# Sparse attention and an ELU layer on one core: scores without padded k, two tiles for q^T and k^T, fillers in batch 0, a new order

## The chip, the core and the metric

The kernel runs on one core of a Trainium2 chip. The core has a matrix engine (TensorE, in profiles PE, with its weight loads as PEld), a vector engine (DVE), a scalar engine (ACT), GpSimd (POOL), a queue engine (SP) and 16 DMA engines. The metric is the time of one execution on the device in microseconds (us); lower is better.

## The reference

Attention over 8 batches, 8 heads, 576 tokens of 64 numbers, with two sparse masks, and then a two-layer network with an ELU over all 4,608 tokens:

```python
scores = scale * np.matmul(q, k.transpose(0, 1, 3, 2))
rel = pos[:, None] - pos[None, :]
mask_local = (rel >= 0) & (rel < 32)                       # heads 0 to 3
mask_strided = (rel >= 0) & (pos[None, :] % 32 == pos[:, None] % 32)   # heads 4 to 7
attn = softmax(np.where(mask, scores, -1e9))
x = (attn @ v).transpose(0, 2, 1, 3).reshape(B * S, H * D)   # 4608 x 512
h = x @ w_in                                                 # 512 -> 2048
g = np.where(h > 0, h, np.exp(np.minimum(h, 0)) - 1)
out = g @ w_out                                              # 2048 -> 512
```

q, k, v and both weights come in float32 and are cast to bf16 as they are loaded; the output is float32.

## The kernel before

**Attention.** Each batch has four strided heads (class s) and four local heads (class l). The token axis is cut into 8 residue classes of 72 tokens for s, and into blocks of 96 for l, so that only blocks that the masks leave are computed. A class has two pairs y of two heads, a pair has two halves u. So a batch has 8 score groups: those of s are eight matmuls of 72 columns, those of l six of 96 columns. A group goes through this chain: scores S (TensorE, L438), exp e (ACT, L445), mask m (DVE), product with v O (TensorE), log of the sums n and reciprocal r (ACT), and x, the product written to xT (DVE). The v tile of the later batches holds columns of ones, so O gives the sums as well.

**q^T and k^T.** In batches 0 to 2 TensorE transposes q and k (T), and a copy brings them to SBUF (c on DVE, C on ACT). From batch 3 on (`NPE = 3`) SP's DMA transposes do this (X, L587). The two heads or residues z of a matmul pair lie in partitions 0 to 63 and 64 to 127 of qT and kT. In batches 0 to 2 a score matmul uses only its 64 partitions, so the two z of a pair lie side by side on the array. From batch 3 on there are two copies `kp` of k^T, in each of which the other 64 partitions are zero, and a score matmul uses all 128 partitions. The copies are filled by two DMAs on SP for each class (P, L593); their zeros are written once at the start, by four copies on ACT (L334) and four small memsets. There is one qT and one kT for each class, so the transposes of a batch wait for the scores of the batch before.

**The network.** Tokens are taken in 9 chunks of 512. For each chunk 16 first-layer rows of four 512-column matmuls (L; in chunk 0 two halves a and b) give h in a PSUM bank; h, i or j and g (exp on ACT, clamp on DVE or ACT, ELU on DVE) write g; then 4 second-layer blocks of four parts with four matmuls each (Z), a copy o (ACT) or q (DVE) into one of two output buffers, and the stores t on SP. A chunk needs all x of the batches that it covers: L.1 those of batches 0 and 1, L.2 of 1 and 2, L.5 of 4 and 5, L.6 of 5 and 6.

**The order.** All work is issued in the order of a long string `ORDER`, a token a step; each engine takes its own steps from it in that order. The names are `S.3l0.1.67` (scores of batch 3, class l, pair 0, half 1, in banks 6 and 7), `D.kl.3` (load k of the local heads of batch 3, on POOL's queue), `X.kl.3` (its DMA transpose, on SP's), `L.2.5.0` (chunk 2, row 5, bank 0), `Z.1.3.0.2` (chunk 1, block 3, part 0, bank 2), `W` and `V` (copies of v), `w.7.42` (42 matmuls of zeros of 128 columns into bank 7), `F` (masks) and `K` (casts of the first q and k). The eight PSUM banks are named in the string by hand.

Of the kernel before, what the change touches and what calls it, by code (L numbers as in the profile page):

```python
# [8 lines left out]
F32 = mybir.dt.float32  # L9
BF16 = mybir.dt.bfloat16  # L10
# [5 lines left out]
S = 576  # L16
D = 64
# [30 lines left out]
T.1l1.q.1 g.0.6 h.0.12 T.1l0.q.5 C.1l1.q i.0.1 a.0.9.6 i.0.12 C.1l0.q T.1l1.k.7 g.0.2 T.1l0.k.1
C.1l1.k g.0.12 T.1s1.k.5 b.0.9 C.1l0.k g.0.1 T.1s0.q.7 D.qs.2 h.0.9 V.1 S.1l1.0.12 S.1l0.1.34
e.1l1.0 b.0.13 c.1s0.q c.1s1.k e.1l0.1 S.1s0.0.12 m.1l1.0 a.0.8.7 h.0.13 m.1l0.1 O.1l1.0.34 e.1s0.0  # L50
i.0.9 a.0.11.5 i.0.13 D.ks.2 n.1l1.0 m.1s0.0 S.1s0.1.12 b.0.8 r.1l1.0 g.0.9 e.1s0.1 b.0.11 x.1l1.0
Z.0.0.0.6 h.0.8 m.1s0.1 h.0.11 g.0.13 O.1s0.0.34 i.0.8 O.1s0.1.12 D.ql.2 n.1s0.0 i.0.11 Z.0.0.1.6
g.0.8 r.1s0.0 n.1s0.1 x.1s0.0 a.0.14.0 r.1s0.1 g.0.11 O.1l0.1.34 b.0.14 x.1s0.1 n.1l0.1 Z.0.2.0.5
h.0.14 D.kl.2 r.1l0.1 i.0.14 Z.0.0.2.6 x.1l0.1 g.0.14 S.1s1.1.34 S.1s1.0.12 e.1s1.1 Z.0.2.1.5
e.1s1.0 m.1s1.1 D.vs.2 Z.0.0.3.6 m.1s1.0 D.vl.2 S.1l0.0.34 o.0.0 S.1l1.1.12 Z.0.3.0.0 e.1l1.1 t.0.0
e.1l0.0 O.1s1.0.67 m.1l1.1 O.1s1.1.12 m.1l0.0 n.1s1.0 O.1l1.1.34 r.1s1.0 Z.0.3.1.0 n.1s1.1 x.1s1.0
n.1l1.1 r.1s1.1 T.2s0.q.6 T.2s0.k.7 r.1l1.1 x.1s1.1 Z.0.3.2.0 C.2s0.q x.1l1.1 c.2s0.k T.2l1.q.6
S.2s0.1.34 c.2l1.q T.2l1.k.7 e.2s0.1 S.2s0.0.12 c.2l1.k O.1l0.0.34 e.2s0.0 T.2l0.k.6 m.2s0.1 n.1l0.0
m.2s0.0 S.2l1.1.12 r.1l0.0 T.2l0.q.7 c.2l0.k e.2l1.1 Z.0.3.3.0 x.1l0.0 C.2l0.q m.2l1.1 L.1.0.4 V.2
o.0.3 W.2 t.0.3 S.2l1.0.67 h.1.0 S.2l0.1.01 T.2s1.q.3 e.2l0.1 T.2s1.k.2 i.1.0 Z.0.2.2.5 D.qs.3  # L60
c.2s1.q e.2l1.0 m.2l0.1 D.ks.3 O.2s0.1.01 c.2s1.k Z.0.2.3.5 g.1.0 n.2s0.1 D.vs.3 m.2l1.0 r.2s0.1
S.2s1.0.67 D.ql.3 q.0.2 O.2s0.0.34 e.2s1.0 L.1.3.2 x.2s0.1 t.0.2 n.2s0.0 Z.0.1.0.7 m.2s1.0 h.1.3
r.2s0.0 i.1.3 O.2s1.0.01 Z.0.1.1.7 g.1.3 n.2s1.0 x.2s0.0 Z.0.1.2.7 r.2s1.0 x.2s1.0 L.1.1.6 D.kl.3
O.2l0.1.01 h.1.1 L.1.6.2 n.2l0.1 i.1.1 Z.0.1.3.7 g.1.1 r.2l0.1 h.1.6 L.1.2.3 x.2l0.1 o.0.1 i.1.6
S.2l0.0.01 D.vl.3 h.1.2 L.1.5.7 t.0.1 g.1.6 e.2l0.0 i.1.2 O.2l1.1.56 X.ql.3 h.1.5 g.1.2 S.2s1.1.01
L.1.7.2 n.2l1.1 i.1.5 m.2l0.0 e.2s1.1 L.1.4.3 g.1.5 h.1.7 X.qs.3 m.2s1.1 r.2l1.1 O.2l0.0.01 i.1.7
Z.1.0.0.7 h.1.4 g.1.7 n.2l0.0 L.1.12.4 i.1.4 x.2l1.1 r.2l0.0 X.ks.3 L.1.8.2 g.1.4 h.1.12 O.2s1.1.56
x.2l0.0 h.1.8 Z.1.0.1.7 W.3 n.2s1.1 X.kl.3 O.2l1.0.01 i.1.12 r.2s1.1 Z.1.3.0.3 i.1.8 n.2l1.0 g.1.12
Z.1.3.1.3 x.2s1.1 r.2l1.0 L.1.13.4 g.1.8 D.qs.4 x.2l1.0 L.1.10.5 h.1.13 i.1.13 L.2.4.6 h.1.10 g.1.13
L.2.10.0 i.1.10 h.2.4 g.1.10 j.2.4 L.2.2.4 h.2.10 g.2.4 L.2.0.5 h.2.2 i.2.10 i.2.2 L.1.14.6 h.2.0  # L70
g.2.10 D.ks.4 P.s.3 L.2.8.2 i.2.0 h.1.14 g.2.2 D.vs.4 j.1.14 L.1.9.0 g.2.0 D.ql.4 h.2.8 g.1.14
L.2.3.1 h.1.9 i.2.8 i.1.9 L.2.1.6 h.2.3 g.2.8 j.2.3 L.1.11.5 g.1.9 X.ks.4 h.2.1 g.2.3 L.1.15.4
h.1.11 i.2.1 D.kl.4 i.1.11 S.3s0.0.01 h.1.15 L.2.5.2 g.2.1 e.3s0.0 P.l.3 i.1.15 L.2.6.6 g.1.11 h.2.5
m.3s0.0 S.3s1.1.01 h.2.6 g.1.15 Z.1.0.2.7 e.3s1.1 i.2.6 D.vl.4 O.3s0.0.45 i.2.5 S.3s0.1.01 m.3s1.1
n.3s0.0 Z.1.3.2.3 g.2.5 e.3s0.1 g.2.6 Z.1.0.3.7 r.3s0.0 m.3s0.1 O.3s1.1.01 x.3s0.0 o.1.0 Z.1.3.3.3
X.kl.4 n.3s1.1 O.3s0.1.45 q.1.3 r.3s1.1 S.3s1.0.67 Z.1.1.0.2 n.3s0.1 x.3s1.1 t.1.0 e.3s1.0 Z.1.1.1.2
r.3s0.1 m.3s1.0 P.s.4 S.3l0.1.67 O.3s1.0.01 x.3s0.1 e.3l0.1 Z.1.1.2.2 X.qs.4 n.3s1.0 W.4 Z.1.1.3.2
m.3l0.1 r.3s1.0 O.3l0.1.67 x.3s1.0 o.1.1 S.3l0.0.45 L.2.9.3 t.1.3 n.3l0.1 e.3l0.0 L.2.15.0 t.1.1
r.3l0.1 m.3l0.0 L.2.12.4 h.2.9 x.3l0.1 h.2.15 O.3l0.0.12 i.2.9 h.2.12 L.2.7.7 i.2.15 n.3l0.0 g.2.9
Z.1.2.0.6 h.2.7 i.2.12 D.qs.5 g.2.15 r.3l0.0 L.2.11.3 D.ks.5 i.2.7 x.3l0.0 D.vs.5 Z.2.0.0.5 h.2.11  # L80
g.2.7 L.2.14.2 i.2.11 g.2.12 Z.2.0.1.5 h.2.14 g.2.11 i.2.14 L.2.13.7 g.2.14 S.3l1.0.34 h.2.13
Z.1.2.1.6 X.ks.5 e.3l1.0 i.2.13 S.4s0.1.01 g.2.13 S.4s0.0.34 e.4s0.1 Z.2.0.2.5 m.3l1.0 m.4s0.1
e.4s0.0 O.3l1.0.01 Z.1.2.2.6 n.3l1.0 m.4s0.0 O.4s0.1.34 r.3l1.0 Z.2.0.3.5 n.4s0.1 x.3l1.0 Z.1.2.3.6
r.4s0.1 q.2.0 x.4s0.1 O.4s0.0.01 o.1.2 t.2.0 Z.2.2.0.7 n.4s0.0 Z.2.2.1.7 t.1.2 r.4s0.0 Z.2.2.2.7
x.4s0.0 Z.2.2.3.7 S.3l1.1.01 o.2.2 Z.2.1.0.2 P.l.4 e.3l1.1 Z.2.1.1.2 m.3l1.1 X.ql.4 O.3l1.1.01
S.4s1.1.67 n.3l1.1 Z.2.1.2.2 e.4s1.1 Z.2.1.3.2 r.3l1.1 t.2.2 m.4s1.1 O.4s1.1.67 x.3l1.1 o.2.1
S.4s1.0.45 Z.2.3.0.3 n.4s1.1 X.qs.5 D.ql.5 e.4s1.0 L.3.10.2 r.4s1.1 m.4s1.0 L.3.1.4 h.3.10 x.4s1.1
P.s.5 L.3.0.5 i.3.10 h.3.1 g.3.10 t.2.1 L.3.3.6 h.3.0 i.3.1 D.kl.5 g.3.1 j.3.0 L.3.8.7 h.3.3 g.3.0
L.3.9.4 h.3.8 i.3.3 i.3.8 L.3.4.5 h.3.9 g.3.3 D.vl.5 j.3.9 L.3.13.2 g.3.8 X.kl.5 h.3.4 g.3.9 L.3.7.7
h.3.13 i.3.4 i.3.13 L.3.2.4 D.qs.6 h.3.7 g.3.4 D.ks.6 L.3.11.6 i.3.7 h.3.2 g.3.13 L.3.15.5 i.3.2  # L90
h.3.11 g.3.7 S.5s0.1.12 i.3.11 h.3.15 L.3.14.0 g.3.2 e.5s0.1 L.3.6.7 g.3.11 h.3.14 m.5s0.1 j.3.15
L.3.12.6 i.3.14 h.3.6 g.3.15 L.3.5.1 h.3.12 i.3.6 X.ks.6 g.3.14 S.4l0.0.45 h.3.5 Z.2.3.1.3 g.3.6
e.4l0.0 i.3.5 Z.2.3.2.3 i.3.12 g.3.5 S.5s1.1.45 g.3.12 S.4l0.1.01 e.5s1.1 Z.2.3.3.3 m.4l0.0 m.5s1.1
e.4l0.1 O.4s1.0.45 O.4l0.0.67 o.2.3 W.5 S.4l1.1.01 Z.3.0.0.2 n.4s1.0 m.4l0.1 t.2.3 D.vs.6 e.4l1.1
Z.3.0.1.2 r.4s1.0 m.4l1.1 O.5s0.1.01 n.4l0.0 x.4s1.0 Z.3.2.0.3 n.5s0.1 r.4l0.0 O.4l0.1.45 Z.3.2.1.3
# [615 lines left out]
```

## Time and profile before

| | |
|---|---|
| runs | 325.38, 326.49, 326.8 us; median 326.49 |
| the profiled execution | 326.53 us, its span 324.7 us |
| PE busy | 308.3 us (95% of the span) |
| DVE, ACT, POOL busy | 227.3, 234.3, 72.3 us |
| first and second layer | 576 matmuls of 512 columns each |
| score matmuls of full rows | 160 of 72 columns, 120 of 96 columns |
| score matmuls of half rows | 96 of 72 columns, 72 of 96 columns |
| mean granted clock of TensorE | 0.972 |
| slower clock, by the trace | 0.5 up to 5.9 us, from 9.3 to 23.0 and from 101.5 to 104.9 |

How to read it: times count from the start of the span. The timeline's lines give start and duration in us, engine, line, operation, tiles, partitions, shape and count, and in brackets the idle time before and what ended it. Matmuls are pipelined: the difference of two starts is what one costs, not its duration. The waits' lines give engine, line, what was waited for, the total in us, how often, and the longest. The windows' lines give for each engine the busy time and the count, then the clock granted to TensorE as a share of full speed, the busy share of the DMA engines (above 1 where packets overlap) and GB/s.

### The profile page before, as it was taken

How to read it: one execution, taken by the hardware profiler on the slowest of the kernel's cores; microseconds unless marked ns; L12 is line 12 of the kernel's file. 1: busy time of each engine (PE TensorE's matmuls, PEld its weight loads, DVE VectorE, ACT ScalarE, POOL GpSimd, SP SyncE). 2: the span in 40 equal slices, each digit the busy share in tenths (PEclk: the TensorE clock that was granted, in tenths of full speed). 3: DMA queues.
4: the chain of work that ended last, by engine and by line, in shares of the span. 5: the costliest groups of instructions: out<-in, count | busy, mean ns of one | idle time of the engine just before them, and what ended most of it. 6: DMA issues, size and time to landing. Idle time of an engine off the chain costs nothing.

```text
span 324.7 us, 6422 instructions
## 1 busy us (share of the span) xinstructions
PE 308.3 (95%) x2410; PEld 158.8 (49%) x2410; DVE 227.3 (70%) x449; ACT 234.3 (72%) x407; POOL 72.3 (22%) x99
## 2 busy tenths in 40 slices
PE   6899999999997999999999989999999999999993
PEld 5754546544453455445544544445545444444441
DVE  7759967889994772896679668951699673850900
ACT  6767968897885876878978879944899756742610
POOL 8534200840750200910075027000000000000000
PEclk9559999999997999999999999999999999999999
DMA  8999999799999866997499969742501101112122
GB/s 172 194 206 197 204 206 137 120 184 124 198 165 172 173 116 163 180 150 142 115 189 121 115 168 92 100 115 81 126 2 32 47 19 33 32 29 56 46 67 66
DMA packets 97455, 39.41 MB, mean 121 GB/s; under 512 B 77936, under 2 KB 91216, under 8 KB 97424
## 3 DMA queue, kind: packets, MB, share of 16 engines
q0 software_dynamic: 64016, 19.40, 56.2%
q1 hardware_dynamic: 33324, 19.46, 27.8%
q8 instruction: 19, 0.31, 0.4%
q10 hardware_dynamic: 84, 0.15, 0.1%
q14 instruction: 12, 0.10, 0.1%
HBM read 39.41 MB, written 9.44 MB: 150 GB/s over the span
## 4 chain that ended last, share of the span: by engine, by line
PE 58%; DVE 14%; ACT 11%; DMA 8%; issue 5%; POOL 2%; SPq 1%; POOLq 0%; DVEq 0%; ACTq 0%
PE ps L634 28%; PE ps L600 22%; DVE g L628 5%; ACT ln L536 4%; PE ps L438 4%; DVE xT L567 4%; DVE he L617 3%; ACT rc L542 3%; DMA qTs<-qs 3%; DMA kpl<-kTl 2%; ACT e L445 2%; DMA ks<-in_k_dram 2%; PE ps L508 1%; DMA qTl<-ql 1%; ACT he L608 1%
## 5 line engine op out<-in xcount | busy, mean ns | idle before, releaser
L634 PE MATMUL ps<-w_out_sb,g 128*128 128x512 bf16 x576 | 137.5, 382 | 0.4 <-DVE g L628 0.3
L600 PE MATMUL ps<-xT,w_in_sb 128*128 128x512 bf16 x576 | 135.7, 381 | 1.7 <-DVE g L628 0.6
L608 ACT ACTIVATE he<-ps 128x512 f32<-128x512 f32 x144 | 83.0, 594 | 26.0 <-PE ps L600 24.2
L600 PEld LDWEIGHTS <-w_in_sb 128*128 128x128 bf16 x576 | 54.5, 98 | 65.0 <-issue 5.9
L628 DVE TENSOR_TENSOR g<-he,ps 128x512 bf16<-128x512 bf16 x118 | 78.6, 679 | 8.6 <-PE ps L634 7.0
L634 PEld LDWEIGHTS <-g 128*128 128x128 bf16 x576 | 53.3, 98 | 57.6 <-issue 1.3
L617 DVE TENSOR_SCALAR he<-he 128x512 bf16<-128x512 f32 x118 | 52.1, 455 | 22.2 <-ACT he L608 21.6
L567 DVE TENSOR_TENSOR xT<-ps,rc 64x576 bf16<-64x576 f32 (+1 forms) x64 | 43.1, 678 | 18.4 <-ACT rc L542 17.5
L445 ACT ACTIVATE e<-ps 72x576 bf16<-72x576 f32 (+1 forms) x64 | 40.4, 646 | 11.4 <-PE ps L438 9.9
L648 ACT COPY osb<-ps 128x512 f32<-128x512 f32 x31 | 18.1, 585 | 36.6 <-PE ps L634 28.9
L536 ACT ACTIVATE ln<-ps 64x576 f32<-64x576 f32 (+1 forms) x64 | 36.9, 582 | 5.6 <-PE ps L508 2.5
L542 ACT ACTIVATE rc<-ln 64x576 f32<-64x576 f32 (+1 forms) x64 | 39.3, 620 | 1.5
L239 POOL DMA_DIRECT2D ql<-in_q_dram x20 | 16.5, 832 | 51.4 <-DMA qTl<-ql 51.4
L452 DVE TENSOR_TENSOR pm<-e,mask_s 72x576 bf16<-72x576 bf16 x32 | 14.3, 450 | 13.4 <-ACT e L445 12.9
L458 DVE TENSOR_TENSOR pm<-e,mask_l 128x576 bf16<-128x576 bf16 x32 | 14.4, 451 | 11.1 <-ACT e L445 11.0
L626 DVE SCALAR_TENSOR_TENSOR g<-he,ps 128x512 bf16<-128x512 bf16 x26 | 17.4, 679 | 0.4 <-ACT he L615 0.2
L615 ACT ACTIVATE he<-he 128x512 bf16<-128x512 f32 x26 | 16.0, 628 | 0.6
L246 POOL DMA_DIRECT2D kl<-in_k_dram x20 | 15.2, 783 | 4.8 <-DMA vs<-in_v_dram 2.5
L233 POOL DMA_DIRECT2D qs<-in_q_dram x7 | 4.8, 688 | 42.9 <-DMA qTs<-qs 24.4
L508 PEld LDWEIGHTS <-vl 128*128 128x128 bf16 x144 | 8.8, 98 | 6.5 <-issue 2.1
L438 PE MATMUL ps<-qTl,kpl 128*128 128x96 bf16 x120 | 8.6, 208 | 2.9 <-DMA kpl<-kTl 1.6
L501 PEld LDWEIGHTS <-vsp 72*128 72x128 bf16 x192 | 9.0, 98 | 4.5 <-issue 0.5
(87 smaller groups left out, 175.8 us busy)
## 6 DMA issues: line engine op xcount, KB each, us to landing
out_dram<-osb SPq DMA_DIRECT2D x31, 144.0 KB
vl<-in_v_dram POOLq DMA_DIRECT2D x8, 288.0 KB, 8.7
w_in_sb<-in_moe_w_in_dram POOLq DMA_DIRECT2D x4, 512.0 KB, 12.6
w_out_sb<-in_moe_w_out_dram POOLq DMA_DIRECT2D x4, 512.0 KB, 15.1
vs<-in_v_dram POOLq DMA_DIRECT2D x6, 320.0 KB, 7.6
qs<-in_q_dram POOLq DMA_DIRECT2D x5, 320.0 KB, 5.8
ks<-in_k_dram POOLq DMA_DIRECT2D x5, 320.0 KB, 7.1
kps<-kTs SPq DMA_DIRECT2D x10, 160.0 KB
```

The lines of the kernel that those rows point to most:

```text
L438: nc.tensor.matmul(dst, lhsT=kt[pr, k0:k0 + 128], rhs=rhs, start=True, stop=True, skip_group_check=True)
L445: nc.scalar.activation(e[0:R], tiles.pop(("S", key, u))[0:R], ACT.Exp, scale=scale)
L536: nc.scalar.activation(t, s_ps, ACT.Ln)
L542: nc.scalar.activation(t, tiles.pop(("ln", key, u)), ACT.Exp, scale=-1.0)
L567: nc.vector.tensor_mul(dst, o_ps, rc)
L600: nc.tensor.matmul(tiles["h", ch, m], lhsT=w_in_sb[:, c, m * 128:(m + 1) * 128], rhs=xT[:, c, ch * CHUNK:(ch + 1) * CHUNK], start=(c == 2) ...
L608: nc.scalar.activation(e, tiles["h", i[0], i[1]], ACT.Exp)
L617: eng.tensor_scalar(e1, e, scalar1=1.0, scalar2=1.0, op0=ALU.min, op1=ALU.subtract)
L626: nc.vector.scalar_tensor_tensor(dst, e1, -1.0, h, op0=ALU.mult, op1=ALU.max)
L628: nc.vector.tensor_tensor(dst, e1, h, op=ALU.max)
L634: nc.tensor.matmul(ops, lhsT=g[ch % 2][:, m, kk * 128:(kk + 1) * 128], rhs=w_out_sb[:, m, :], start=(m == 0), stop=(m == MC - 1), skip_gro ...
L648: eng(o_sb, o_ps)
```

## The change

The padded copies `kp` are gone, with their zeros and the step P. All score matmuls use 64 partitions, the two z of a pair side by side. qT and kT exist twice, and even and odd batches take turns. The zeros of k^T's borders are set in both. The fillers write columns 384 to 511 of a bank, and 83 of them are added in batch 0's part of the order. The order is another one from end to end: other banks, another place for nearly each step, and in chunk 1 to 6 the attention of several batches interleaved. The numbers of matmuls, exps, masks, loads, transposes and stores are the same.

```diff
-    qT = {c: consts.tile([128, 2 * NS * RP], BF16, tag=f"qT{c}", name=f"qT{c}") for c in "sl"}
-    kT = {"s": consts.tile([128, KSW], BF16, tag="kTs", name="kTs"),
-          "l": consts.tile([128, KLW], BF16, tag="kTl", name="kTl")}
-    kp = {(c, z): consts.tile([128, kT[c].shape[1]], BF16, tag=f"kp{c}{z}", name=f"kp{c}{z}")
-          for c in "sl" for z in range(2)}
+    qT = [{c: consts.tile([128, 2 * NS * RP], BF16, tag=f"qT{c}{i}", name=f"qT{c}{i}")
+           for c in "sl"} for i in range(2)]
+    kT = [{c: consts.tile([128, n], BF16, tag=f"kT{c}{i}", name=f"kT{c}{i}")
+           for c, n in (("s", KSW), ("l", KLW))} for i in range(2)]
...
-    for y in range(2):
-        nc.vector.memset(kT["s"][:, y * KSY + NS * RS:(y + 1) * KSY], 0.0)
-    nc.vector.memset(kT["l"][:, 0:PRE], 0.0)
-    for (c, z), t in kp.items():
-        s_ = slice(2 * NS * RP, None) if c == "s" else slice(0, PRE)
-        nc.vector.memset(t[z * D:(z + 1) * D, s_], 0.0)
-        r = slice((1 - z) * D, (2 - z) * D)
-        w = t[r].bitcast(F32)
-        nc.scalar.copy(w, zero[r, 0:2].bitcast(F32).to_broadcast([D, w.shape[1]]))
+    for t in kT:
+        nc.vector.memset(t["s"][:, NS * RS:KSY], 0.0)
+        nc.vector.memset(t["s"][:, KSY + NS * RS:], 0.0)
+        nc.vector.memset(t["l"][:, 0:PRE], 0.0)
...
+            self.qT, self.kT = qT[self.b % 2][self.c], kT[self.b % 2][self.c]
...
-        def rows(self, z):
-            return slice(z * D, (z + 1) * D) if self.pe else slice(0, 128)
...
-            nc.tensor.matmul(ps[:, int(bank), 0:128], lhsT=zero, rhs=zero, start=True, stop=True,
+            nc.tensor.matmul(ps[:, int(bank), 384:512], lhsT=zero, rhs=zero, start=True, stop=True,
...
-                pr = P.rows(z)
-                kt = kT[P.c] if P.pe else kp[P.c, z]
+                pr = slice(z * D, (z + 1) * D)
...
-                    rhs = qT["s"][pr, q0:q0 + RS]
+                    rhs = P.qT[pr, q0:q0 + RS]
...
-                nc.tensor.matmul(dst, lhsT=kt[pr, k0:k0 + 128], rhs=rhs, start=True, stop=True,
+                nc.tensor.matmul(dst, lhsT=P.kT[pr, k0:k0 + 128], rhs=rhs, start=True, stop=True,
...
-            out_, in_ = qT[c], raw["q" + c]
...
+        t = (qT if nm == "q" else kT)[int(b) % 2][c]
...
-    def pad_k(c, b):
-        s_ = slice(0, NS * 2 * RP) if c == "s" else slice(PRE, KLW)
-        for z in range(2):
-            r = slice(z * D, (z + 1) * D)
-            nc.sync.dma_start(out=kp[c, z][r, s_], in_=kT[c][r, s_])
```

Some places of the new order. Its beginning, up to the first halves b of chunk 0:

```
w.7.42 F.ms K.q.0 K.q.1 D.wi0.0 F.ml T.0s0.q.0 K.k.0 D.wi1.0 c.0s0.q K.k.1 w.7.5 T.0s1.q.7 D.wi2.0
c.0s1.q w.7.5 T.0s0.k.0 T.0s1.k.1 D.wi3.0 c.0s0.k c.0s1.k w.7.6 S.0s0.0.67 S.0s0.1.45 e.0s0.0
S.0s1.0.01 S.0s1.1.23 D.qs.1 e.0s1.1 m.0s0.0 e.0s1.0 w.7.13 O.0s0.0.67 m.0s1.1 e.0s0.1 O.0s1.1.23
m.0s1.0 D.ks.1 T.0l0.q.0 n.0s0.0 m.0s0.1 n.0s1.1 O.0s1.0.45 c.0l0.q r.0s0.0 r.0s1.1 x.0s0.0 w.7.3
O.0s0.1.01 n.0s1.0 x.0s1.1 D.vs.1 T.0l0.k.6 r.0s1.0 T.0l1.k.7 n.0s0.1 x.0s1.0 r.0s0.1 T.0l1.q.2
c.0l0.k C.0l1.k x.0s0.1 w.7.6 S.0l0.1.34 D.ql.1 S.0l0.0.56 V.0 e.0l0.1 c.0l1.q e.0l0.0 m.0l0.1
w.7.14 S.0l1.0.01 S.0l1.1.23 m.0l0.0 e.0l1.0 O.0l0.1.45 O.0l0.0.67 e.0l1.1 m.0l1.0 n.0l0.1 w.7.4
O.0l1.0.01 m.0l1.1 n.0l0.0 r.0l0.1 D.kl.1 w.7.3 a.0.1.2 r.0l0.0 x.0l0.1 a.0.0.3 n.0l1.0 x.0l0.0
a.0.2.4 r.0l1.0 a.0.3.7 x.0l1.0 O.0l1.1.56 n.0l1.1 D.vl.1 r.0l1.1 x.0l1.1 w.6.24 b.0.3 a.0.4.5 h.0.3
```

The first row of chunk 1, and the loads, transposes and first scores of batch 3 (lines with "..." leave steps out):

```
S.2l1.1.23 x.2s0.1 Z.0.0.3.7 e.2l1.1 m.2l1.1 O.1l1.1.12 o.0.0 O.2l1.1.34 n.1l1.1 S.2l0.1.56 t.0.0
n.2l1.1 T.2s1.q.7 Z.0.3.3.0 c.2s1.q r.1l1.1 D.qs.3 r.2l1.1 x.1l1.1 T.2s1.k.7 o.0.3 L.1.1.2 c.2s1.k
...
h.1.3 i.1.4 L.1.6.4 i.1.3 h.1.7 g.1.4 S.2s1.1.56 i.1.7 h.1.6 S.2s1.0.01 D.kl.3 g.1.3 L.1.8.2 e.2s1.0
...
O.2s1.0.45 L.1.13.6 g.1.8 n.2l0.1 i.1.5 n.2s1.0 L.1.9.2 g.1.12 D.vl.3 X.ql.3 r.2l0.1 g.1.5 L.1.11.7
r.2s1.0 x.2l0.1 h.1.13 Z.1.0.0.3 x.2s1.0 h.1.11 D.qs.4 h.1.9 i.1.11 S.2l0.0.01 S.2l1.0.45 D.ks.4
i.1.13 e.2l0.0 Z.1.0.1.3 i.1.9 g.1.11 L.1.14.0 g.1.9 X.kl.3 L.1.15.7 g.1.13 h.1.14 m.2l0.0 Z.1.0.2.3
...
O.2l1.0.01 t.1.0 S.3s1.1.45 n.2l1.0 S.3l0.0.23 Z.1.2.0.7 e.3l0.0 r.2l1.0 m.3l0.0 S.3s0.0.23
```

Batch 4 has the same sequence further on: `D.vl.4 x.3s1.1 X.ql.4`, `D.qs.5`, `D.ks.5`, `X.kl.4`, then `o.1.3 ... t.1.3`, and its first scores `S.4s0.1.56 ... S.4l1.1.34`.

## The prediction

> **What bounds the kernel now.** First the page's busy shares and costliest groups.
>
> ```profile
> span 324.7 us, 6422 instructions
> PE 308.3 (95%) x2410; PEld 158.8 (49%) x2410; DVE 227.3 (70%) x449; ACT 234.3 (72%) x407; POOL 72.3 (22%) x99
> L634 PE MATMUL ps<-w_out_sb,g 128*128 128x512 bf16 x576 | 137.5, 382 | 0.4 <-DVE g L628 0.3
> ```
>
> TensorE is the bound; the other engines have a quarter of the span free. But 382 ns is a pipelined duration. What one instruction costs is the distance from one start to the next, so I read the timeline of PE next (start, duration, count). Its first rows are of batch 1 and 2, where scores are already side by side, then come rows of batch 3 with padded k:
>
> ```profile
> 58.55 0.42 PE L501 MATMUL ps<-pm,vsp 72*128 72x72 bf16 x8
> 58.81 1.03 PE L634 MATMUL ps<-w_out_sb,g 128*128 128x512 bf16 x4
> 59.77 0.30 PE L438 MATMUL ps<-qTs,kTs 64*128 64x72 bf16 x8
> 60.01 0.43 PE L501 MATMUL ps<-pm,vsp 72*128 72x72 bf16 x8
> ...
> 93.19 0.43 PE L438 MATMUL ps<-qTs,kps 128*128 128x72 bf16 x8
> 93.45 1.89 PE L634 MATMUL ps<-w_out_sb,g 128*128 128x512 bf16 x8
> ```
>
> Four 512-column matmuls take 0.863 us where others of full rows follow. Eight full-row 72-column matmuls take 0.26 us (58.55 to 58.81, and 93.19 to 93.45), six of 96 columns 0.255. A side-by-side group starts 0.96 us after a group of four, 0.095 late, and itself lasts 0.24 where four pairs of 32 ns are 0.13: some 0.095 again before the next full-row matmul. So each change between full rows and half rows costs 0.095 us.
>
> With these prices I added up the matmuls in program order. From 21.41 us (the stream of first-layer matmuls) to the last start at 319.3 lie 297.9 us: 279.0 of array time, 39 changes of 0.095 (3.7) and 15.2 of waiting and slow clock. The waits of PE name the largest pieces:
>
> ```profile
> PE ps L438 <- DMA kpl<-kTl: 1.6, 1, 1.6
> PE ps L438 <- DMA qTl<-ql: 1.3, 1, 1.3
> ```
>
> ```profile
> 98.74 0.20 PE L438 MATMUL ps<-qTl,kpl 128*128 128x96 bf16 x1
> 100.58 0.39 PE L438 MATMUL ps<-qTl,kpl 128*128 128x96 bf16 x5 [1.64 <-DMA kpl<-kTl]
> ...
> 101.06 3.22 PE L634 MATMUL ps<-w_out_sb,g 128*128 128x512 bf16 x8
> 104.08 0.68 PE L508 MATMUL ps<-pm,vl 128*128 128x96 bf16 x6
> ```
>
> After the first wait eight matmuls take 3.02 us instead of 1.73: the granted clock was 0.5 from 101.5 to 104.9. By starts, the waits for transposed or padded q and k (89.4, 98.3, 98.7, 190.9) come to 3.9 us and the slow clock after them to 1.3. Slow clock at 21.4 to 23 is 0.8; 9.2 stay in small waits for exp, x and g.
>
> Last the windows of the beginning (PE, PEld, DVE, ACT, POOL, clock, DMA):
>
> ```profile
> 9.00:10.00 1.00, 0.61 (x22) 0.61 (x24) 0.70 (x2) 0.14 (x1) 1.00 (x2) 0.66 1.22 201
> 19.00:20.00 1.00, 1.00 (x9) 0.28 (x8) 0.83 (x2) 1.00 (x4) 0.00 (x0) 0.50 1.25 216
> 23.00:24.00 1.00, 1.00 (x6) 0.49 (x5) 0.00 (x0) 0.00 (x0) 0.14 (x1) 1.00 1.24 206
> ```
>
> The clock is 0.5 from 9.3 to 23.0, while ACT is nearly full: it works 11.6 of the 12.55 us from 9.86 to 22.41. Batch 0's attention is bound by ACT.
>
> **The change part by part.** The sum is made against the profiled execution, 326.53 us (span 324.7), beside a median of 326.49.
>
> *Scores side by side.* Batches 3 to 7 have 40 score groups, 20 of 0.26 and 20 of 0.255: 10.3 us. Side by side they are 0.13 each, 5.1: -5.2. But 23 stretches of half rows arise there (11 single groups, 7 of two, 5 of three), 46 changes; batches 1 and 2 have three fewer. 43 x 0.095 = +4.1. A single group thus costs 0.32 against 0.26, a pair 0.44 against 0.51. Sum **-1.1**.
> The Trainium skill, "TensorEngine Tiling (Array Packing)", section Theoretical Speedup, gives up to 2x for 64 rows; its Key Properties say that changing the tiling mode drains the engine. By the speed-up alone this step would be -5.2; the trace agrees with the drain and gives its price, 0.095.
>
> *No padding.* SP loses 20 DMAs of about 0.59 us issue, 11.8 in all, and a score waits for one transfer instead of two. With two tiles for q^T and k^T a transposition no longer waits for the scores of the batch before: in the order, counted in array time, the q and ks transpositions of batches 3 and 4 now stand 10 to 19 us ahead of their first scores, ks of batch 5 stands 7.3 ahead; batches 6 and 7 have 16 us or more. The four waits of 3.9 us and the 1.3 of slow clock go: **-5.2**. What is late next is k of the local heads: X.kl.3 stands 6.1 us before S.3l0.0, X.kl.4 5.9 before S.4l1.1. How long does such a transposition take? By the trace's packets, from issue to last packet, 2.7 (at 100.74), 3.6 (79.74), 4.8 (201.35), 7.1 (140.72) and 10.4 (173.95). It is slow where loads run beside it:
>
> ```profile
> 136.11 1.18 POOL L256 DMA_DIRECT2D vl<-in_v_dram  x1
> ...
> 138.27 0.66 POOL L233 DMA_DIRECT2D qs<-in_q_dram  x1
> 138.92 0.72 POOL L233 DMA_DIRECT2D ks<-in_k_dram  x1
> ```
>
> ```profile
> 140.72 3.23 SPq L587 DMA_TRANSPOSE kTl<-kl  x1
> ```
>
> The new order has just this sequence (D.vl, D.qs, D.ks, then X.kl) in both batches, so I take 7.1: waits of 1.0 and 1.2, **+2.2**. Ends: 0 (the 4.8 row, under the lead) and 11.4 (the 10.4 row twice, 4.3 + 4.5, each with 1.3 of slow clock). SP holds t.1.3 behind X.kl.4; its output buffer is wanted again some 10 us later (o.2.0), so this costs nothing unless X.kl.4 takes longer than that. On POOL the loads of batch 3 stand 4 to 7 us of array time later, most of the others earlier, by up to 19 (ql of batch 5); POOL's longest waits (51.4 us for qTl, 24.4 for qTs) are for buffers that now come free earlier, and no engine but SP waits behind them.
>
> *The beginning.* Four zero copies of 0.7 us leave ACT at 2.1 to 5.0; ACT then waited 0.58 for a DMA, so nothing is gained. On DVE four memsets (0.38) go, three (0.19) come. The second transposition no longer waits 0.55 for its bank. Scores start some 0.5 earlier. ACT gets one more copy (C.0l1.k, 0.67). So ACT ends near 22.4 and the first b at 22.8, with four a behind it; before, four a and one b were done at 24.0. At 0.43 a pair, 2.8 b are done by then: 1.8 more, **-0.8**. That needs the full clock. Fillers after the first 42 are 83 of 128 columns, 0.056 each at full clock, 4.6 us, in the roughly 4 us of PE's gaps between 5.7 and 21.4 and in the time that real matmuls save at full clock. Ends -1.5 and +2.6 (rival two).
>
> *Order anew.* The end is alike: a copy on ACT and three store DMAs, some 5 us after the last matmul. In between I looked where a first-layer row waits for the last x of its batches. At L.1.1 the chain after the second-layer group is o 0.585, n 0.643 twice, r 0.679, x 0.753, with 0.2 of passing on 3.5 us; PE has 2.4 queued (0.4 + 0.26 + 0.32 + 0.26 + 0.86 + 0.26): a wait of 1.1. At L.5.1 the same count gives 0.6, at L.2.5 and L.6.9 0.3 each; 2.3 in all, where the old order waited 1.2 at such places (0.53 of it at 163.8). **+1.1**. DVE's work, added up by durations, is 24.9 us on 21.2 of PE in chunk 1; its starts lie 0.08 closer than its durations, which takes some 3.7 off about 45 instructions, so DVE is at par there and PE stays the bound. The old order's worst stretch was 24.2 on 21.8. Three more copies of transposes go from DVE to ACT (0.65 each); ACT has 90 us free. So the rest of the 9.2 stays; it may be 3 either way, since every position has moved.
>
> Sum: -1.1 - 5.2 + 2.2 - 0.8 + 1.1 = -3.8, so **322.7 us**.
>
> **Rivals.** *One: kT comes late.* In the 173.95 row loads ran all the while beside the transposition. If both X.kl go so, the waits cost 11.4 instead of 2.2: +5.4, 331.9 us. It ends slower by 0.5% from 7.6 us of such waits. Against it: the new order spreads loads and transpositions more evenly, and the old clump of four at 71 to 80 is gone.
> *Two: the clock stays at half through batch 0.* Scores, transposes and fillers from 5.9 to 9.3 still leave gaps; the clock fell at 9.3 after a stretch with PE's matmuls in under half of it. Then the fillers take 9 us and stand in the way, until a full stretch of 3.4 us brings the clock back, as at 19.6 to 23.0. Two such stretches at half speed lose 3.4: +2.6 instead of -0.8, 326.1 us.
> The Trainium skill, "TensorE: Matmul & The Clock Gate", Why this matters for your kernels, asks only for no idle gaps above some 3 us; by it no clock would have fallen after the 1.64 us wait, and the removed 1.3 would not be counted (324.0). The row decides.
> *Three: the new order also waits less elsewhere.* Scores now run further ahead of their batch (the first of batch 5 at 101 us of array time, before at 117), so exp and x have longer to come. If X.kl is in time and 3 of the 9.2 go instead of 1.1 coming: -1.1 - 5.2 - 0.8 - 3 = -10.1, 316.4 us. Against it: nothing in the profile says which small waits go.
>
> **How the numbers follow.** Forecast 0.47 (own range 320 to 325), rival one 0.13 (from 328 to 332), two 0.17, three 0.20, something unseen 0.03, taken as slower. A range of 316.5 to 328 leaves out most of one and half of three, some 0.2. This kernel's measurement can tell about 0.5% from no change (324.9 to 328.1): faster 0.67, same 0.17, slower 0.16.
>
> **What would show it.** Half-row groups at L431 with 0.095 at both edges and scores near 8 us instead of 13 in all; no wait for qT; short waits for kTl near 85 and 107 us; clock 1.0 from about 6 us on; no 0.5 at 101. I am wrong if waits for kTl exceed 3 us each, if 0.5 stands in the windows from 9 to 23, or if DVE's and ACT's small waits grow beyond 12 us.

## The result and the profile after

The changed kernel took 339.51 us (median of 334.95, 339.29, 339.74, 339.77) against 325.94 for the kernel before: a ratio of 1.038, with a 95% interval from 1.029 to 1.047. I had forecast 322.7 us. The profiled execution is the fastest of the four, 334.95 us with a span of 333.0; a second profile of the same kernel, in the first experiment, is one of 340.82.

The page of after, shares, the row of PE and of its clock over 40 slices of 8.3 us:

```profile
span 333.0 us, 6534 instructions
PE 306.5 (92%) x2454; PEld 156.3 (47%) x2493; DVE 223.6 (67%) x444; ACT 233.9 (70%) x407; POOL 72.6 (22%) x99
...
PE   6899999999549999799999999999999999999994
...
PEclk9799999999959999999999999999999999999999
```

PE is still the bound, but the row has a hole in slices 11 and 12 (83 to 100 us), with the clock down right behind it. The waits of PE name it (total in us, times, longest):

```profile
PE ps L431 <- DMA kTl<-kl: 8.1, 1, 8.1
PE ps L431 <- DMA kTs<-ks: 1.9, 1, 1.9
...
PE ps L373 <- ACT kTl L407: 0.9, 1, 0.9
```

L431 are scores, L373 the matmuls of zeros (fillers). Timeline of PE around the wait:

```profile
87.44 0.31 PE L431 MATMUL ps<-qTs,kTs 64*128 64x72 bf16 x8
95.80 0.42 PE L431 MATMUL ps<-qTl,kTl 64*128 64x96 bf16 x6 [8.05 <-DMA kTl<-kl]
...
98.33 1.89 PE L621 MATMUL ps<-w_out_sb,g 128*128 128x512 bf16 x4
```

The first local scores of batch 3 (S.3l0.0) wait 8.05 us, once, for X.kl.3. Behind it four second-layer matmuls take 1.7 us (98.33 to 100.01) instead of 0.863: the granted clock is 0.5 from 90.5 to 100.8. The chain that ended last, in order of time, shows how X.kl.3 came to be so late:

```profile
65.73 10.19 DMA vs<-in_v_dram
...
76.20 7.37 DMA kl<-in_k_dram
...
83.72 12.03 DMA kTl<-kl
```

k of the local heads stands late among the batch's loads on POOL, behind those of q, k, v of the strided heads and of q; it lands at 83.6. Then the transposition takes 12.0 us. In before it took 3.6 (79.74 to 83.31, by its packets), and POOL issued nothing from 70.75 to 82.29. SP, then POOL, of before:

```profile
79.74 2.14 SPq L587 DMA_TRANSPOSE kTl<-kl  x1
```

```profile
70.75 0.74 POOL L258 DMA_DIRECT2D vl<-in_v_dram  x1
82.29 0.66 POOL L233 DMA_DIRECT2D qs<-in_q_dram  x1 [10.80 <-DMA qTs<-qs]
```

What ran beside it in after is in the timelines of SP and of POOL:

```profile
80.11 1.58 SPq L580 DMA_TRANSPOSE qTl<-ql  x1
83.72 2.77 SPq L580 DMA_TRANSPOSE kTl<-kl  x1
...
90.30 3.83 SPq L580 DMA_TRANSPOSE qTs<-qs  x1
```

```profile
80.66 0.66 POOL L233 DMA_DIRECT2D qs<-in_q_dram  x1 [0.44 <-issue]
83.79 0.64 POOL L233 DMA_DIRECT2D ks<-in_k_dram  x1 [2.47 <-DMA kTs<-ks]
86.23 0.64 POOL L233 DMA_DIRECT2D vs<-in_v_dram  x1 [1.80 <-DVE vsp L567]
91.37 3.23 POOL L239 DMA_DIRECT2D ql<-in_q_dram  x4 [4.50 <-DMA qTl<-ql]
```

The loads and X.qs.4 belong to batch 4; X.ql.3 stands just ahead of X.kl.3 on SP's queue. A load of batch 4 waits only until batch 3's transposition, or the copy of v, has read its buffer (the brackets of POOL). X.qs.3 and X.ks.3 had done so by 83.8 us, while kl landed late; so the loads run beside the one transposition that PE is about to need. The second tile can have a part in it: X.qs.3 is issued at 68.61, ahead of the last strided scores of batch 2 (71.14), for which it would have waited with one tile, as X.qs.4 would for scores of batch 3. No run has the new order with one tile, so the second tile's part and the order's are not separated.

The beginning, in the windows that were shown of before (PE, PEld, DVE, ACT, POOL, clock, DMA):

```profile
9.00:10.00 1.00, 1.00 (x18) 1.00 (x16) 0.69 (x2) 0.00 (x0) 1.00 (x2) 0.50 1.23 203
19.00:20.00 1.00, 0.97 (x22) 0.70 (x18) 0.67 (x3) 1.00 (x3) 0.33 (x1) 1.00 1.19 198
23.00:24.00 1.00, 0.65 (x12) 0.65 (x12) 0.20 (x1) 0.74 (x2) 0.19 (x1) 1.00 1.24 205
```

After the first 5 us the clock is 0.5 only from 8.6 to 12.0 (before: 9.3 to 23.0), and yet the tenth half row of the first layer starts at 26.63 us (its first weight load); before it was 25.41.

### The profile page after: what moved, and what is told of

Same layout as the page of the kernel before. It is cut to its first block, busy times and chain, and to the rows that moved or that the text cites. A ratio compares the mean times of both kernels' runs of the same rounds, so it can differ in the third digit from the quotient of the medians.

```text
span 333.0 us, 6534 instructions
## 1 busy us (share of the span) xinstructions
PE 306.5 (92%) x2454; PEld 156.3 (47%) x2493; DVE 223.6 (67%) x444; ACT 233.9 (70%) x407; POOL 72.6 (22%) x99
## 4 chain that ended last, share of the span: by engine, by line
PE 50%; DMA 17%; ACT 14%; issue 9%; DVE 7%; POOL 2%; SPq 0%; POOLq 0%; ACTq 0%; DVEq 0%
PE ps L621 23%; PE ps L587 22%; DMA qs<-in_q_dram 5%; ACT ln L529 4%; DMA kTl<-kl 4%; ACT rc L535 3%; DMA kTs<-ks 3%; DMA vs<-in_v_dram 3%; ACT he L595 2%; DMA kl<-in_k_dram 2%; PE ps L431 2%; DVE g L615 2%; DVE xT L560 2%; ACT e L438 2%; DVE he L604 2%
## 5 line engine op out<-in xcount | busy, mean ns | idle before, releaser
L621 PE MATMUL ps<-w_out_sb,g 128*128 128x512 bf16 x555 | 134.2, 382 | 2.4 <-issue 1.3
L587 PE MATMUL ps<-xT,w_in_sb 128*128 128x512 bf16 x558 | 129.5, 379 | 2.1 <-DVE g L615 0.4
L595 ACT ACTIVATE he<-ps 128x512 f32<-128x512 f32 x144 | 84.1, 595 | 29.1 <-PE ps L587 27.5
L604 DVE TENSOR_SCALAR he<-he 128x512 bf16<-128x512 f32 x119 | 50.7, 438 | 23.0 <-ACT he L595 22.6
L438 ACT ACTIVATE e<-ps 72x576 bf16<-72x576 f32 (+1 forms) x64 | 39.6, 646 | 20.1 <-PE ps L431 18.6
L635 ACT COPY osb<-ps 128x512 f32<-128x512 f32 x33 | 19.3, 585 | 30.0 <-PE ps L621 21.7
L431 PE MATMUL ps<-qTl,kTl 64*128 64x96 bf16 x192 | 9.0, 206 | 9.0 <-DMA kTl<-kl 8.1
L256 POOL DMA_DIRECT2D vl<-in_v_dram x8 | 9.5, 1193 | 30.4 <-PE ps L501 22.0
L233 POOL DMA_DIRECT2D vs<-in_v_dram x7 | 4.8, 685 | 51.2 <-DVE vsp L567 49.3
L373 PE MATMUL ps<-zero 128*128 128x128 bf16 x125 | 11.4, 256 | 3.5 <-DVE zero L295 1.1
```

The source lines that it names most:

```text
L438: nc.scalar.activation(e[0:R], tiles.pop(("S", key, u))[0:R], ACT.Exp, scale=scale)
L587: nc.tensor.matmul(tiles["h", ch, m], lhsT=w_in_sb[:, c, m * 128:(m + 1) * 128], rhs=xT[:, c, ch * CHUNK:(ch + 1) * CHUNK], start=(c == 2) ...
L595: nc.scalar.activation(e, tiles["h", i[0], i[1]], ACT.Exp)
L604: eng.tensor_scalar(e1, e, scalar1=1.0, scalar2=1.0, op0=ALU.min, op1=ALU.subtract)
L621: nc.tensor.matmul(ops, lhsT=g[ch % 2][:, m, kk * 128:(kk + 1) * 128], rhs=w_out_sb[:, m, :], start=(m == 0), stop=(m == MC - 1), skip_gro ...
L635: eng(o_sb, o_ps)
```

## The experiments

My theory after the result: the new order's loss is transpositions that run beside loads, above all X.kl.3, and the slow clock behind such waits; the changed code itself is sound. Rivals: the code parts (scores side by side, two tiles, no padding) cost time; the fillers cost it; the new order is worse in its many small waits. "Ratio" is to the kernel before, with its 95% interval; the last column is the profiled execution's start of the tenth half row.

| run | median, us | ratio | waits for kT in the profile | tenth half |
|---|---|---|---|---|
| a0, after unchanged | 339.93 | 1.042 [1.035, 1.049] | kTl 14.0, kTs 1.5 | 26.96 |
| a1, loads of batch 4 held | 331.39 | 1.020 [1.014, 1.025] | kTl 1.2 + 3.5 | 28.65 |
| a4, k of local heads first | 330.39 | 1.010 [1.005, 1.016] | kTs 2.4 | 27.05 |
| a2, fillers in other banks | 337.05 | 1.032 [1.024, 1.040] | kTl 10.8, kTs 1.1 | 26.95 |
| a3, no fillers | 334.4 | 1.021 [1.012, 1.029] | kTl 7.0, kTs 2.1 | 25.68 |
| b1, changed code, old order | 322.22 | 0.991 [0.987, 0.995] | none | 24.92 |
| c1, before with two tiles | 326.36 | 0.998 [0.994, 1.003] | padded k 0.4 | 25.26 |
| d1, b1 with full-row scores | 322.44 | 0.988 [0.981, 0.994] | none | 24.91 |
| b2, b1 with the fillers | 325.44 | 0.996 [0.993, 1.000] | none | 29.91 |
| a5, a4 without fillers | 326.62 | 1.000 [0.996, 1.005] | kTs 3.4 | 25.75 |
| a6, a5 with X.ks.5 alone | 322.62 | 0.990 [0.985, 0.994] | kTs 0.8 | 24.68 |
| b3, b1 once more | 323.27 | 0.992 [0.989, 0.996] | none | 26.02 |

**After once more (a0).** No edit.

> The changed kernel once more. The profiled execution took 334.95 us and three others 339.3 to 339.8, so a wait must differ from execution to execution. Theory (transposes slowed by loads beside them): the time is 335 to 340, and where it is near 339.5 the wait for kTl of batch 3 is as long as 8.1 us or longer, or a second wait for a transposed tile of over 3 us stands beside it. Rival (TensorE's clock): the wait is the same 8.1 us and the difference lies in longer stretches at clock 0.5 that no long wait precedes.

Measured: 339.93 us; in its profile the transposition of kl took 18.7 us (issue at 83.12, scores at 101.8), and PE waited 14.0, as the theory had it:

```profile
83.12 18.66 DMA kTl<-kl
```

The spans of the two profiles of after differ by 5.8 us (338.8 and 333.0), their waits for kTl by 6.0: that one transposition accounts for the difference between these two executions.

**The transposition without the loads beside it (a1).** On POOL D.kl.4, which has to wait for X.kl.3, now stands ahead of D.qs.4 and D.ks.4 and so holds them:

```diff
-x.2s1.0 h.1.11 D.qs.4 h.1.9 i.1.11 S.2l0.0.01 S.2l1.0.45 D.ks.4 i.1.13
+x.2s1.0 h.1.11 h.1.9 i.1.11 S.2l0.0.01 S.2l1.0.45 i.1.13
...
-g.1.9 X.kl.3 L.1.15.7
+g.1.9 X.kl.3 D.kl.4 D.qs.4 D.ks.4 L.1.15.7
...
-h.2.0 r.3s0.0 D.kl.4 Z.1.2.1.7
+h.2.0 r.3s0.0 Z.1.2.1.7
```

> D.kl.4 is moved to just behind X.kl.3 and D.qs.4 and D.ks.4 behind it, so POOL's queue stands at D.kl.4 until the transposition of kl of batch 3 has read its source, and no load of batch 4 runs beside it. Theory (the loads of batch 4, which come free early because q^T and k^T have two tiles, slow the transposition): X.kl.3 takes 3 to 6 us from issue to landing instead of 12.0, the wait at S.3l0.0 falls from 8.1 to under 2.5 us, no clock 0.5 follows, and the time falls by 6 to 10 us, to 327 to 331. Rival (k of the local heads is loaded too late, its landing at 83.6 us decides): X.kl.3 is faster but the wait stays over 5 us. Second rival (SP's own four transpositions in a row slow each other): X.kl.3 stays over 9 us.

Chain of a1:

```profile
84.41 6.82 DMA kTl<-kl
```

The same transposition, issued at nearly the same time, takes 6.8 us instead of 12.0 and 18.7 (I had expected 3 to 6), and the time falls by 0.022 of before (7.2 us) against a0 on the same chip. So what ran beside it made it slow. Holding the loads also put X.qs.4 off, from 90.30 to 100.09, so the run alone does not part loads from transposition. X.kl.3 still comes 1.2 us late, because kl lands as late as in after, and X.kl.4 now comes 3.5 late, behind loads that were held.

**k of the local heads first (a4).** The other way out: loads stay as they are, but D.kl and X.kl of batches 3 and 4 (and those of ql) go ahead of those of the strided heads (and are taken out at their old places).

```diff
-T.2l1.q.1 n.2s0.0
+T.2l1.q.1 D.kl.3 D.ql.3 n.2s0.0
...
-h.1.2 g.1.1 X.qs.3 L.1.10.4
+h.1.2 g.1.1 X.kl.3 X.ql.3 X.qs.3 L.1.10.4
...
-x.2s1.0 h.1.11 D.qs.4
+x.2s1.0 h.1.11 D.kl.4 D.ql.4 D.qs.4
...
-S.3s0.0.23 Z.1.1.3.6 X.qs.4
+S.3s0.0.23 Z.1.1.3.6 X.kl.4 X.ql.4 X.qs.4
```

> The changed kernel with the local heads first: D.kl.3 and D.ql.3 stand just behind the last transposition of batch 2's local heads, X.kl.3 and X.ql.3 ahead of X.qs.3, and the same for batch 4. POOL was idle from 41 to 63 us, so these loads start near 56. Theory (the short lead of kT of the local heads beside loads is what costs the time): no wait for kTl over 1 us in batches 3 and 4, no clock 0.5 between 25 us and the end, and the time is 324 to 328. A new wait for kTs of batch 3 may take its place, since qs and ks still stand at T.2s1: up to 3 us, then 328 to 331. Rival (the new order waits elsewhere too): 331 us or more without a wait for a transposed tile of over 3 us.

Measured: 1.010, that is 0.028 (9.1 us) below after. The wait for kTl and the slow clock near 90 us are gone, but the median is at the upper end of what I expected; what is left as a DMA wait in the profile is kTs, of batch 5 and not of batch 3:

```profile
PE ps L431 <- DMA kTs<-ks: 2.4, 1, 2.4
```

**The fillers (a2, a3, b2, a5).** a2 moves six of the ten groups of fillers to banks that nothing reads at that time, such as `w.7.5` to `w.3.5` (twice) and `w.6.24` to `w.0.24`. a3 leaves all 83 added ones out:

```diff
-K.k.1 w.7.5 T.0s1.q.7 D.wi2.0 c.0s1.q w.7.5 T.0s0.k.0
+K.k.1 T.0s1.q.7 D.wi2.0 c.0s1.q T.0s0.k.0
```

and so on for the other eight places.

> Five of the fillers write to other banks (3 and 0), which no copy or ACT instruction is about to read; number and place stay. Theory (the fillers of the changed kernel wait for readers of their own bank, 0.8, 0.9 and 0.6 us in the waits of PE, and hold up the steps behind them): the first scores start at 9.4 instead of 10.3 us, the first b at 23.5 instead of 24.6, some 1 us less in all. Rival (ACT bounds the beginning, the fillers' waits lie beside it): the first b moves by under 0.3 us. The wait at S.3l0.0 stays near 8 us in both.

> The changed kernel without the 83 fillers of batch 0; the first 42 stay. The changed kernel reached its tenth half of a first-layer row at 26.6 to 27.0 us, the kernel before at 25.4, the changed code in the old order, without fillers, at 24.9. Theory (the fillers wait for readers of their bank and hold up batch 0 by more than the clock gains): the tenth half comes at 25 to 26 us, 1 us or more earlier, although the clock is 0.5 for most of 9 to 22 us. Rival (the fillers do their work; the new order of batch 0 with its copy of kTl on ACT costs the time): the tenth half comes at 27 us or later. The wait at S.3l0.0 stays at 8 to 14 us in both, so the whole time is near 337 to 340.

In a2 the first scores start 1.4 us earlier than in after (8.94 and 10.30), since the fillers no longer wait for the readers of their bank; at the tenth half row nothing of it is left (26.95). So the theory on these waits fell: they lie beside other work. In a3 the clock is at 0.5 until 21.9 us, and the tenth half row still starts 1 us earlier than in after. One such milestone tells little, since it varies by 1.1 us between profiles with the same beginning (b1 and b3, a5 and a6); but in the new order all five profiles with the fillers lie at 26.6 or later, the three without them at 25.8 or earlier. Both medians carry the kTl wait with its changing length, so I took the fillers to places without it: b2 adds them to b1, a5 takes them out of a4.

> The changed code in the order of before (322.2 us in its own run, clock 0.5 from 8.0 to 21.6 us), with the changed order's 83 matmuls of zeros put at the like places of batch 0. Theory (matmuls of zeros wait for the readers of their own bank, so that they gain nothing): the clock stays at 1.0 over more of the beginning, and yet the tenth first-layer half of chunk 0 comes no earlier than 24.9 us, rather 0.5 to 1.5 later; median 322 to 324 us. Rival (the full clock is worth what step 'the beginning' of the prediction says): the tenth half comes at 23.5 to 24.1 us, median near 321 us.

> The changed order with k of the local heads loaded and transposed first (330.4 us) and without the 83 matmuls of zeros. If these cost what the run without them alone showed in the milestones, the tenth first-layer half comes near 26 us instead of 27.05 and the median is near 329.4 us; the rest of the distance to the old order's 322.2, some 7 us, then lies in the new order after batch 0. Rival (they earn their time by the clock): clock 0.5 through the beginning costs 2 us and more, median 332 us or above.

a5 is faster than a4 (1.000 against 1.010, 3.2 us, give or take 2.3). b2 is slower than b1 by its median (0.996 against 0.991 and, on a third chip, 0.992), but these intervals overlap. Both rivals, by which the full clock pays for the fillers, fall. Not all of the 3.2 us need be the fillers: the recorded mean clock of a4's other executions is 0.974 to 0.984, against 0.993 in its profile, so they may hold a longer wait for kTs of batch 5. In the two profiles PE comes to that wait at 124.25 us in a4 and at 121.90 in a5, 2.35 earlier without the fillers. The timeline of PE shows how they cost, first b1, then b2, at the same place:

```profile
17.72 0.50 PE L478 MATMUL ps<-pm,vl 128*64 128x96 bf16 x6
18.20 0.42 PE L430 MATMUL ps<-qTl,kTl 64*128 64x96 bf16 x6
```

```profile
17.59 0.50 PE L479 MATMUL ps<-pm,vl 128*64 128x96 bf16 x6
18.07 1.65 PE L373 MATMUL ps<-zero 128*128 128x128 bf16 x14
19.65 0.42 PE L431 MATMUL ps<-qTl,kTl 64*128 64x96 bf16 x6
```

In b2 the clock had fallen at 16.2 us in spite of the fillers, so fourteen of them last 1.6 us and stand ahead of scores that ACT needs. ACT, which sets the pace of batch 0, waits:

```profile
20.11 0.65 ACT L438 ACTIVATE e<-ps 128x576 bf16<-128x576 f32 x1 [1.82 <-PE ps L431]
```

A fixed count of fillers is not "matmuls in gaps": PE takes them in order, whether there is a gap or not. This profile of b2 is one of its longer executions (327.34 us, median 325.44). In the seven of twelve with a recorded mean clock of 0.992 or more b2 took 323.4 to 326.2 us, so it gained nothing on b1's 321.6 to 324.5 there either. The sizes missed what I had expected: b2's median is above 322 to 324, a5's below 329.4.

**The code without the order (b1, c1, d1).** b1 is the changed code with before's order (P steps left out, no added fillers). c1 is before with only the two tiles for q^T and k^T. d1 is b1 with the scores of batches 3 to 7 over all 128 partitions again, where without padding each sums over both z, so that only its time is of use:

```diff
-                pr = slice(z * D, (z + 1) * D)
+                pr = slice(z * D, (z + 1) * D) if P.pe else slice(0, 128)
```

> The changed code (two tiles for q^T and k^T, no padded copies, all scores side by side) in the order of the kernel before, without the steps P and without fillers. Array time by the prices of the kernel before: scores -5.2, 70 more changes between full and half rows +6.7, so +1.5. Theory (the parts are sound, the new order's short lead of X.kl.3 costs the time): the waits for kpl, kps and qTl (3.9) and the slow clock after them (1.3) go, 322 to 325 us. Rival (half rows cost more than priced, or early loads collide with transpositions in any order): 328 us or more.

> The kernel before, with its order and its padded copies, and with two tiles each for q^T and k^T: one part of the change alone. Theory (the two tiles give back what the transpositions waited for, the padding costs the rest): the wait for qTl at 190.9 (1.5 us) goes, those for kpl and kps at 89 to 99 us (2.4, and 1.3 of slow clock) stay: 324 to 325.5. Rival (most of the gain of the changed code in the old order comes from the second tile): 321.5 to 323, as there. Second rival (earlier loads disturb the padding's DMAs): 326.5 or more.

> The changed code in the old order, but the scores of batches 3 to 7 use all 128 rows of q^T and k^T, so that each sums over both z: the number and shape of the matmuls are those of the padded kernel, the values of the output are not the reference's. By the prices, scores +5.2 and 70 changes less, -6.7: 1.5 us faster than the half rows in the same order (322.2), so 320 to 321.5. Rival (side by side is worth more than the changes of shape cost): slower than 322.2. Rival (a change of shape costs more than 0.095 each): under 319.5.

b1 is faster than before, by 0.9% (interval 0.5 to 1.3). So the code is sound and the order loses 0.047 against it (15.4 us). c1 is the same as before: with the padding DMAs in place, the second tile gives nothing in the median. d1 equals b1: side by side or over full rows, the scores cost the same within this measurement. c1 (326.4) and d1 (322.4) both lie above what I had expected of them, 324 to 325.5 and 320 to 321.5. c1 and d1, on one chip, differ in the padding and its zeros, and by 0.011 (3.5 us): what b1 gains comes with the padding's end, with two tiles in place. The padding's end with one tile was not run.

**The last transposition (a6), and b1 again (b3).** The profile of a5 has one DMA wait left, and it is of the same kind. Chain of a5, then POOL's timeline:

```profile
115.11 10.12 DMA kTs<-ks
```

```profile
106.14 1.10 POOL L232 DMA_DIRECT2D qs<-in_q_dram  x1 [15.77 <-DMA qTs<-qs]
107.52 0.64 POOL L232 DMA_DIRECT2D ks<-in_k_dram  x1 [0.28 <-issue]
...
108.78 3.29 POOL L238 DMA_DIRECT2D ql<-in_q_dram  x4
112.06 1.57 POOL L245 DMA_DIRECT2D kl<-in_k_dram  x2
```

Batch 5's loads come in one clump once X.qs.4 has freed the buffer, and X.ks.5 (issued at 115.11, behind X.qs.5) runs beside those of ql and kl. PE waits 3.4 us and the clock goes to 0.5 for 6.8. In a6 the loads of ql and kl stand behind two that wait for X.qs.5 and X.ks.5:

```diff
-x.3s1.0 o.1.2 D.ql.5 L.2.4.7
+x.3s1.0 o.1.2 L.2.4.7
...
-r.4l1.1 X.ks.5 g.2.9
+r.4l1.1 X.ks.5 D.qs.6 D.ks.6 D.ql.5 D.kl.5 g.2.9
```

(D.kl.5, D.qs.6 and D.ks.6 are taken out at their old places further on.)

> The changed order with k of the local heads first and without the 83 matmuls of zeros (326.6 us; in its profile PE waited 3.4 us for kTs of batch 5, whose transposition was issued at 115.1 and took some 10 us beside the loads of ql and kl of batch 5, and the clock was at 0.5 from 124.5 to 131.3). Now the loads D.ql.5 and D.kl.5 stand on POOL behind D.qs.6 and D.ks.6, which wait for X.qs.5 and X.ks.5, so that X.ks.5 has few loads beside it. Theory (all that the new order loses after batch 0 is transpositions beside loads, and the clock that falls after the waits): the wait goes, the clock does not fall near 125, 3.4 + 3.4 = 6.8 us less in the profile (321 us), median 321 to 323.5. Rival (the order is worse in its small waits too): the DMA waits go and the median stays above 324.5 us.

> The changed code in the order of before once more, on the same chip as the run beside it: 322 us again (ratio 0.991, between 0.987 and 0.995), if that gain does not depend on the chip. If it does, the ratio lies outside that interval.

POOL of a6:

```profile
120.64 0.64 POOL L232 DMA_DIRECT2D ks<-in_k_dram  x1 [0.46 <-issue]
121.27 3.28 POOL L238 DMA_DIRECT2D ql<-in_q_dram  x4
```

X.ks.5, issued at 115.6, has its last packet at 119.6: 4.0 us, where by packets it took 9.1 in a5. The wait is gone (0.8 us for kTs of batch 3 is left), no fall of the clock is recorded after 19.9 us until PE is done, and the median is 322.62. The rival, that the new order is also worse in its small waits, falls: a6 and b1 are equal (0.990, and 0.991 and 0.992) within 0.5%. a6 and b1 are both faster than before, by 1%, and than after.

So the loss can be followed, in this order of steps: 1.038 (after), less 0.028 for k of the local heads in time (a4), less 0.010 for the fillers (a5), less 0.011 for X.ks.5 (a6), is 0.990. The three are 9.1, 3.2 and 3.5 us, the last two each within some 2 us.

## Why the prediction was wrong

*Scores side by side, -1.1.* The prices hold. In a6 a single group starts 0.96 us after the four matmuls ahead of it and 0.23 ahead of the next full rows:

```profile
111.71 1.02 PE L620 MATMUL ps<-w_out_sb,g 128*128 128x512 bf16 x4
112.67 0.30 PE L430 MATMUL ps<-qTl,kTl 64*128 64x96 bf16 x6
112.90 1.90 PE L586 MATMUL ps<-xT,w_in_sb 128*128 128x512 bf16 x8
```

0.96 less 0.863 is 0.097. But b1 against d1 shows no gain in the time; a step of 1.1 us is below what these intervals tell.

*No padding, -5.2.* The sign is right, the size half to two thirds: 3.5 us from c1 to d1. With the side-by-side step I had -6.3, and b1 and b3, which hold both, gained 0.009 and 0.008 of before, 2.9 and 2.5 us. I had taken one execution's four waits as gone from each execution. That may be the reason, though it is not shown: b3's profile (324.92 us) again has a wait of 1.4 for qTl, and one of 1.9 for exp, that b1's (321.62) has not.

*X.kl, +2.2: the step that failed.* I wrote "X.kl.3 stands 6.1 us before S.3l0.0 ... so I take 7.1". Both numbers were wrong in the same direction. The lead was 4.0: PE was ready at 87.75 and the transposition was issued at 83.72, because it stood behind its load and not behind its place in the order. The load was late since qs, ks, vs and ql stand ahead of it on POOL; I had counted POOL's moved loads at nothing. And it took 12.0 to 18.7 us, not 7.1. I had bounded it by the slowest row of before (10.4), and chosen the 7.1 row for its neighbours on POOL *in the order*. But neighbours in time are set by when buffers come free: here it stood behind X.ql.3 on SP's queue, and the loads of batch 4 ran beside it. I had read the freed buffers as only a gain ("for buffers that now come free earlier, and no engine but SP waits behind them"). 12.0 less 4.0 is the wait of 8.0.

So rival one was the mechanism, and its argument against ("the new order spreads loads and transpositions more evenly") was wrong. Its size fell short, 331.9 against 339.5: it priced two X.kl at 10.4, where one took 12.0 to 18.7 and X.kl.4 brought no wait, and it left out kTs of batch 5, of which I had written that it stands 7.3 us ahead; it took 9 to 11.

*The beginning, -0.8.* It was +1.2 (25.41 to 26.63), with the full clock from 12.0 us on. Without the fillers it is +0.3 in the new order (a3) and -0.7 in a6's profile, both at half clock to about 20 us. So rival two had the sign and, for after, the wrong cause: the clock was full, and the fillers took PE's time all the same, on an engine that already had to serve ACT in time. Their waits for the readers of their bank (the 0.9 above, and 0.8 for a copy of q^T) did not decide it, by a2. I had written that they lie "in the roughly 4 us of PE's gaps".

*Order anew, +1.1.* With its DMAs in time and no fillers the new order costs as much as the old one, within 0.5% (a6 against b1 and b3).

*The slow clock.* I let a row of 1.64 us decide against a page. The Trainium skill, "TensorE: Matmul & The Clock Gate", section Why this matters for your kernels, asks for no idle gap above some 3 us. In these runs the clock fell in waits of 14.0, 10.8, 8.1, 7.0, 3.5 (a1) and 3.4 us (a5), and not after 1.9 (after), 2.4 (a4) or 1.2 (a1): eight second-layer matmuls behind the waits of after and a4 take the full-clock 1.7 us. So the page fits all of these waits but the row of before, which had another wait just ahead (98.3); why that one fell is open.

## What to carry to other kernels

When a change frees a buffer or moves a load, ask which transfers will now start earlier and what they will run beside: here a load set loose early was harmless only where no transfer that an engine was about to need ran at that time. Price a DMA by the rows with the traffic that the new order will allow, count its lead from when its own load lands, count what stands ahead of it on its queue, and put the load and the transposition that are wanted first in front on their queues. Dummy matmuls that keep a clock up are ordinary work on an in-order engine: in these runs 83 of them in fixed places gained nothing.

## What the runs showed of the hardware

*A DMA transposition beside loads is slower by a factor of three to five.* From issue to landing, 295 KB of k (4 heads of 576 times 64 in bf16) took 3.6 us in before (to its last packet), and to the release of the scores 6.8 in a1, 12.0 in after, 18.7 in a0. Part of this is its place on SP's queue. Counted in order of issue (1,152 packets for a transposition of kl, 1,280 for each other, 24,960 in all), its first packet comes 2.5 us after its issue in before, 3.4 in a1, 4.2 in after and 5.3 in a0, when the transposition ahead of it is done. Its own packets then take 1.1 us in before, 1.4 in a1, 7.2 in after and 8.6 or more in a0.

The Trainium skill, "DMA: Bandwidth & Descriptors", section Latency and other measured facts, gives 261 GB/s as effective for such transpositions; that would be 1.1 us, an estimate, and the packets in before agree with it. These windows show what the DMA engines moved while the transposition's packets ran, in before, after and a0 (the last two numbers are the busy share and GB/s):

```profile
82.00:83.00 1.00, 1.00 (x6) 0.49 (x5) 1.00 (x3) 1.00 (x3) 0.66 (x1) 1.00 1.28 287
```

```profile
88.00:90.00 2.00, 0.00 (x0) 0.00 (x0) 0.00 (x0) 0.01 (x1) 0.00 (x0) 1.00 1.72 77
```

```profile
92.00:94.00 2.00, 0.00 (x0) 0.00 (x0) 0.00 (x0) 0.00 (x0) 2.00 (x3) 0.50 1.51 39
```

In after and a0 the engines were no less busy and moved 77 and 39 GB/s instead of 287. So the packets took longer; it was not that the bytes of the loads filled the time. Which of the neighbours slows them, and how, was not separated.

*The recorded clock moves in steps of 3.41 us.* Around the waits and in batch 0 it was at 0.5 for 10.24 us in after, 17.07 in a0, 6.83 in a5, 13.65 in b1: 3, 5, 2 and 4 of them.

*The recorded clock can be missing a fall.* The windows from 11 to 13 us of b1 and then of b3, the same kernel (the clock is third from the right):

```profile
11.00:13.00 2.00, 1.67 (x36) 1.50 (x37) 1.59 (x4) 1.92 (x5) 1.11 (x2) 0.50 2.31 160
```

```profile
11.00:13.00 2.00, 1.68 (x37) 1.51 (x38) 1.59 (x4) 1.92 (x5) 0.98 (x2) 1.00 2.33 163
```

The same busy time, and the same two 288-column matmuls of 0.45 us at 11.28 in both timelines; at full clock (after, 12.54) two such take 0.31. So b3 ran at half clock there, whatever its record says, and a clock is to be checked against durations before an argument rests on it.
